# Division of the exponentials of two more batches moved to GpSimd, in a sliding-window attention with a GELU layer

## The chip, the cores and the metric

The kernel runs on one core of a Trainium2 chip. The metric is the device time of one execution in microseconds (us). Engines are called TensorE (PE; its weight loads PEld), VectorE (DVE), ScalarE (ACT), GpSimd (POOL) and SyncE (SP, which issues the DMAs).

## What is computed

```python
# q, k, v: [8, 8, 576, 64] (batch, head, position, feature); w_in [512, 2048], w_out [2048, 512], all float32
scores = scale * np.matmul(q, k.transpose(0, 1, 3, 2))
mask = (rel >= 0) & (rel < 128)                       # rel = query position - key position
scores = np.where(mask, scores + bias[None], -1e9)    # bias: -slope of the head * rel
attn = np.exp(scores - np.max(scores, axis=-1, keepdims=True))
attn = attn / (np.sum(attn, axis=-1, keepdims=True) + 1e-09)
x = np.matmul(attn, v)                                # to [4608, 512]: heads side by side
h = x @ w_in
out = 0.5 * h * (1.0 + erf(h / sqrt(2))) @ w_out      # float32
```

## The kernel before

**Numbers as halves.** Most products are made in float16 with three terms: each float32 operand is scaled by a power of two and split into a high half (the value rounded to float16) and a low half (the rest); high by high, low by high and high by low are added in PSUM. `low_part` (L334, one VectorE instruction at L335) makes a low half as source x scale - high.

**Attention, by units.** A unit is one batch and one pair of heads: 8 x 4 units. A unit's scores are 9 groups of 128 rows (two heads' or two blocks' queries, 64 each) by 192 keys. The steps of a unit of batch 1 or later: `scores` (L634, matmuls of 64 rows into PSUM), `biased` (L686: VectorE scales and adds the bias into `s`, float32 in SBUF; GpSimd fills masked stretches at L699), then for the groups 0 to 4 and 5 to 8 apart `softmax` (L776: maxima at L781, one exponential a group on ScalarE at L785 with its row sum, reciprocal of the sums at L788 and L789, then the division), `low_weights` (L799: the low halves and the transpose, a DMA from `e_main` to `et` at L809), at last `weigh` (L826: matmuls of `et` with the halves of v, L854) and `leave` (L862: two halves of x). `e_main` is one tile for all units, `s` and `et` are two each.

**The division has two forms**, chosen by a letter for each batch in `HALVES` (L36). Form "a" (L792): ScalarE copies each group with the scale 1/sum to the high half in `e_main`, and VectorE makes its low half from `s`, the scale and the high half, group by group (L808, recorded as L335). Form "w": GpSimd multiplies each group of `s` by 1/sum in place (L795); ScalarE casts all 5 or 4 groups at once to the high halves (L797); VectorE subtracts these from `s` in one instruction (L805). Batch 0 is done in float32 in another way and ignores its letter. Before, batches 1 and 2 have form "a" and batches 3 to 7 form "w".

**The layers.** Tiles of 512 tokens go through w_in (L904 in the first tiles; later in seven smaller products with precomputed sums, L1133), GELU on ScalarE, halves (GpSimd or ScalarE high, VectorE low) and w_out (L950, L947 in float32 for tile 0, L1283 for the last tiles). The precomputed sums are written to DRAM and loaded again. From batch 3's time on `qbuf`, `kbuf`, `vbuf` and `e_main` hold q, k, v and the exponentials, and at the end, when the attention is over, sums of weights.

**The order is written out.** Each piece of work is a generator, and each `next` of it (a step) issues its instructions. `ORDER` (L62) lists the steps of the whole kernel, 3570 of them, and the engines get their instructions in that order. The first digit is a stage, then come a letter and the unit or part: `0M30` is a step of `softmax` of batch 1, unit 3, groups 0 to 4, `0N30` one of its `low_weights`, `0Y3` its weighing; batch 2 has `02M30`, `02N30` and `02Y3`, batch b from 3 on the digit b - 1 (`4M30` for batch 5). `0z0` to `0z2` load q and k of batch 0, `0F` w_in, `0H3` is a part of the first layer's product, `0g3` its GELU. `PSUM_BANKS` and `ROOMS` say which PSUM bank and which output room each request gets, in the order of the requests. Engines wait for each other by semaphores, set from the tiles that each instruction reads and writes.

**Places.** Tiles in SBUF lie in the order in which they are first asked for, each rounded up to 32 bytes a partition. `one` (L287) is a tile of one element for a matmul that spreads a maximum over the partitions (L300). In the program of the kernel before `qbuf` begins at byte 6688 of each partition, `kbuf` at 15904, `vbuf` at 25632 and `e_main` at 35872.

Of the kernel before, what the change touches and what calls it, by code (L numbers as in the profile page):

```python
# [11 lines left out]
F32 = mybir.dt.float32  # L12
# [23 lines left out]
HALVES = "aaawwwww"  # L36
# [31 lines left out]
0n20 0j0 0n20 0n20 0t1 0e1 0x30 0t1 0n21 0t1 0n21 0a1 0p0 0w0 0e1 0e1 0t1 0e1 0t1 0e1 0z 0p0 0j1 0t2 0t2 0F 0p0 0p0
0n30 0z 0z 0v0 0p0 0W0 0e2 0e2 0F 0n30 0p0 0j1 0m31 0n21 0t2 0e2 0t2 0n21 0j1 0F 0n21 0t2 0F 0F 0e2 0v0 0W1 0L1 0v0
0v0 0i0 0a2 0m31 0v0 0e2 0v0 0n30 0n30 0n30 0n30 0x31 0a2 0i0 0l0 0l0 0L0 0i1 0w1 0l1 0l1 0w2 0H1 0x31 0H1 0t3 0t3  # L70
0x31 0x31 0n31 0H0 0n31 0H0 0i1 0l2 0a3 0H2 0n30 0n31 0n31 0t3 0n31 0n31 0l2 0a3 0j2 0p1 0a4 0a4 0j2 0e3 0e3 0e3 0t3
0t3 0H3 0H3 0p1 0e3 0e3 0H1 0p1 0p1 0w3 0H2 0j4 0a5 0j5 0W3 0j2 0p1 0d 0l3 0j4 0F 0p1 0W2 0L2 0lv 0lv 0lv 0H3 0i2 0a5
0p2 0f 0l3 0H2 0H0 0lv 0i2 0L3 0f 0j3 0H1 0p0 0g1 0p2 0H2 0g2 0p2 0p2 0H4 0j4 0H3 0p2 0j5 0p2 0j3 0H5 0H5 0H4 0p1 0j6
0a6 0a7 0j7 0H4 0H4 0p2 0i4 0i4 0H5 0H5 0g5 0H8 0H8 0H8 0H8 0g8 0j3 0H9 0H9 0H9 0H9 0g9 0j5 0i5 0i3 0H0 0g0 0v1 0a7
0a6 0p3 0i5 0H10 0A0 0i3 0A1 0J1 0H10 0J0 0H11 0j6 0H11 0H11 0p3 0v1 0H6 0H11 0g11 0H7 0v1 0j6 0H6 0p3 0p3 0H10 0H10
0p3 0p3 0i6 0p3 0v1 0v1 0v1 0u1 0cl 0H6 0cl 0j7 0f 0cl 0g3 0i6 0A2 0J2 0H7 0H7 0H7 0g7 0H12 0H12 0H13 0H13 0j7 0H12
0H12 0g4 0A1 0g12 0H13 0H13 0i7 0i7 0lq 0q1 0H15 0H15 0g10 0A0 0A2 0H6 0J0 0J0 0lq 0J1 0J1 0H14 0v1 01c 0H14 0H14 0H14
# [129 lines left out]
def attention_gelu_mlp(  # L207
# [10 lines left out]
    nc = tc.nc  # L218
# [68 lines left out]
    one = pool.tile([1, 1], F32, name="one")  # L287
# [1229 lines left out]
```

## Time and profile before

| what | us |
|---|---|
| median of 3 runs | 874.44 (871.98 to 876.07) |
| profiled execution, its time | 873.86 |
| profiled execution, its span (first to last instruction) | 872.1 |
| TensorE busy | 842.9 (97%) |
| VectorE busy | 706.8 (81%) |
| ScalarE busy | 612.0 (70%) |
| GpSimd busy | 342.9 (39%) |

The profile is one execution. Busy times are unions of the engine's instructions; matmuls overlap, so a busy TensorE is one that always has a matmul under way. The clock granted to TensorE is full (1.00) but for the last window, after the last matmuls. Batches 1 and 2 fill the stretch from about 100 to 250 us, the other batches that up to about 720 us; after that only the layers of the last tiles are left.

### The profile page before, as it was taken

The numbers are of one execution on the slowest core, as the hardware profiler recorded it, in microseconds if no ns is written. First come the engines' busy times: TensorE is split into PE (matmuls) and PEld (weight loads), VectorE is DVE, ScalarE is ACT, GpSimd is POOL, SyncE is SP. The second block draws the span as 40 slices with busy tenths as digits, with TensorE's granted clock in tenths as the row PEclk, the third lists the DMA queues.
The fourth block names the chain that finished last, engine by engine and source line by source line (L and its number), as shares of the span: only waits on it lengthen the run. The fifth ranks groups of instructions, "written<-read, shape, count | busy, mean of one in ns | idle before, by whom it ended". The sixth has DMA issues, their size and how long they took to land.

```text
span 872.1 us, 19752 instructions
## 1 busy us (share of the span) xinstructions
PE 842.9 (97%) x7876; PEld 549.3 (63%) x7876; DVE 706.8 (81%) x1275; ACT 612.0 (70%) x1234; POOL 342.9 (39%) x553
## 2 busy tenths in 40 slices
PE   7899999999999999999999998998999999999997
PEld 4644444544544455884578556864587467888886
DVE  5998999899889966889797988799778656784772
ACT  6978879888769967775677776764776547753671
POOL 5731000033024774479635965576435670000000
PEclk9999999999999999999999999999999999999999
DMA  9855666642563557555846396447752493412301
GB/s 306 286 161 201 230 188 116 152 161 57 102 144 98 137 133 207 194 128 150 188 143 187 104 212 177 127 86 188 187 188 56 110 200 152 188 50 85 110 1 50
DMA packets 180940, 129.47 MB, mean 148 GB/s; under 512 B 134384, under 2 KB 157040, under 8 KB 177136
## 3 DMA queue, kind: packets, MB, share of 16 engines
q1 hardware_dynamic: 180848, 128.21, 53.3%
q8 instruction: 62, 1.02, 0.5%
q14 instruction: 30, 0.25, 0.1%
HBM read 75.89 MB, written 17.83 MB: 107 GB/s over the span
## 4 chain that ended last, share of the span: by engine, by line
PE 55%; DVE 19%; DMA 10%; ACT 8%; issue 4%; POOL 3%; SPq 0%; DVEq 0%; ACTq 0%; POOLq 0%
PE u L1133 12%; PE v L1133 9%; PE h L904 9%; DMA et<-e_main 7%; PE o L950 6%; PE o L947 5%; PE u_out L1283 4%; DMA k<-kp 3%; DVE g L335 3%; PE sc L667 3%; DVE s L693 2%; DVE e_main L805 2%; DVE nmax L781 2%; PE av L854 1%; PE z_out L1283 1%
## 5 line engine op out<-in xcount | busy, mean ns | idle before, releaser
L950 PEld LDWEIGHTS <-g 128*128 128x128 f16 x1152 | 111.0, 98 | 131.2
L950 PE MATMUL o<-wo,g 128*128 128x512 f16 x864 | 192.2, 379 | 0.0
L785 ACT ACTIVATE s<-s,nmax 128x192 f32<-128x192 f32 x252 | 112.0, 446 | 46.8 <-DVE nmax L781 46.5
L904 PE MATMUL h<-x,wi 128*128 128x512 f16 x576 | 128.6, 379 | 1.9 <-DVE wi L335 1.6
L795 POOL TENSOR_SCALAR s<-s,z 128x192 f32<-128x192 f32 x180 | 100.9, 576 | 25.0 <-DVE z L789 11.5
L1133 PEld LDWEIGHTS <-t 128*128 128x128 f16 x1008 | 98.4, 98 | 11.8
L904 PEld LDWEIGHTS <-wi 128*128 128x128 f16 x576 | 54.8, 98 | 67.8 <-DVE wi L335 1.9
L1133 PEld LDWEIGHTS <-wi 128*128 128x128 f16 x864 | 83.9, 98 | 13.4 <-issue 1.3
L699 POOL MEMSET s<- 64x128 f32 (+1 forms) x112 | 19.3, 173 | 157.2 <-DVE s L693 143.6
L693 DVE SCALAR_TENSOR_TENSOR s<-sc,cs,bias_h 128x384 f32<-128x384 f32 x112 | 65.6, 606 | 2.0 <-PE sc L667 1.1
L950 PE MATMUL o<-wo_moved,g 128*128 128x512 f16 x288 | 66.0, 379 | 0.0
L781 DVE TENSOR_REDUCE nmax<-s 128x5 f32<-128x960 f32 (+1 forms) x56 | 58.4, 1047 | 3.4 <-POOL s L699 2.5
L1133 PE MATMUL u<-xs,t 128*128 128x256 f16 x504 | 59.9, 273 | 0.0
L947 PE MATMUL o<-zo,g 128*128 128x512 f32 x128 | 57.6, 599 | 0.0
L854 PE MATMUL av<-et,vbuf 128*64 128x128 f16 (+2 forms) x1392 | 43.7, 220 | 13.7 <-DMA et<-e_main 13.7
L805 DVE TENSOR_TENSOR e_main<-s,e_main 128x960 f16<-128x960 f32 (+1 forms) x40 | 46.5, 1168 | 11.4 <-ACT e_main L797 11.3
L667 PE MATMUL sc<-kbuf,qbuf 64*64 64x192 f16 (+3 forms) x1656 | 49.3, 251 | 6.3 <-DMA kbuf<-kp 4.6
L854 PEld LDWEIGHTS <-vbuf 128*64 128x64 f16 x1392 | 40.3, 111 | 23.4 <-issue 17.9
L1184 POOL TENSOR_SCALAR g<-rooms,sg 128x512 f16<-128x512 f32 x48 | 39.5, 830 | 24.7 <-ACT rooms L1178 21.5
L785 ACT ACTIVATION_READ_ACCUMULATOR s<-s,nmax 128x1 f32 x252 | 47.7, 189 | 0.0
L335 DVE SCALAR_TENSOR_TENSOR g<-rooms,sg,g 128x512 f16<-128x512 f32 x48 | 40.6, 864 | 8.0 <-POOL g L1184 7.9
L797 ACT CAST e_main<-s 128x960 f16<-128x960 f32 (+1 forms) x40 | 36.1, 907 | 14.5 <-POOL s L795 10.4
(256 smaller groups left out, 1698.6 us busy)
## 6 DMA issues: line engine op xcount, KB each, us to landing
t<-stored SPq DMA_DIRECT2D x21, 1024.0 KB, 5.2
v<-vp SPq DMA_DIRECT2D x32, 320.0 KB, 5.4
out<-ob SPq DMA_DIRECT2D x34, 256.0 KB, 2.8
raw<-w_in SPq DMA_DIRECT2D x8, 1024.0 KB, 10.7
raw<-w_out SPq DMA_DIRECT2D x8, 1024.0 KB, 6.1
q<-qp SPq DMA_DIRECT2D x7, 1152.0 KB, 5.8
k<-kp SPq DMA_DIRECT2D x7, 1152.0 KB, 7.1
stored<-sums SPq DMA_DIRECT2D x8, 512.0 KB, 2.7
```

Source lines behind the costliest of these rows:

```text
L335: return nc.vector.scalar_tensor_tensor(out=dst, in0=src, scalar=scale, in1=high, op0=ALU.mult, op1=ALU.subtract)
L667: done = nc.tensor.matmul(ps[bank][o, n, gap:W], a, m[:, gap:W], start=(i == 0 and (n == 0 or b > 0)), stop=(i == len(terms) - 1 and b > 0 ...
L693: yield nc.vector.scalar_tensor_tensor(out=s[:, bank[0] : bank[0] + k, :], in0=ps[bank][:, 0:k, 0:W], scalar=cs, in1=bias.broadcast_to([P, ...
L781: yield nc.vector.tensor_reduce(out=nmax[:, r], in_=s[:, r], axis=AX.X, op=ALU.max, negate=True)
L785: yield nc.scalar.activation(s[:, i, :], s[:, i, :], AF.Exp, bias=nmax[:, i : i + 1], accum_out=z[:, i : i + 1])
L795: yield nc.gpsimd.tensor_scalar(to, s[:, i], z[:, i : i + 1], 1.0, op0=ALU.mult, op1=ALU.mult)
L805: yield engine.tensor_tensor(out=e[:, r, 1, c], in0=st.s[:, r], in1=e[:, r, 0, c], op=ALU.subtract)
L854: done = nc.tensor.matmul(av[r, (js[0] - blocks[0]) * QB : (js[-1] + 1 - blocks[0]) * QB], v32s[b][:, hp, kb, r] if b < EXACT else vbuf[:, ...
L904: done = nc.tensor.matmul(ph, wi[n][:, a, cc, k * P : (k + 1) * P], x[:, cc, b, :], start=(i == 0), stop=(i == 3 * NCC - 1),)
L947: done = nc.tensor.matmul(o, g[:, r, c], zo[n][:, n % 2, k * DM : (k + 1) * DM], start=(fc == first), stop=(fc == last))
L950: done = nc.tensor.matmul(o, g[:, r, a, c], (wo if t else wo_first)[n][:, b, k, :], start=(fc == first and i == 0), stop=(fc == last and i ...
L1133: done = nc.tensor.matmul(ps[:, k * HT : (k + 1) * HT], w(a, i)[:, k * P : (k + 1) * P], m(b, i), start=first and n == 0, stop=True, skip_ ...
```

## The change

`HALVES` gives batches 1 and 2 the letter "w". Their nine scaled copies and nine scaled subtractions a unit become nine divisions on GpSimd, two casts and two subtractions. The instructions of all other work are the same. `ORDER` (now 3530 steps), `PSUM_BANKS` and `ROOMS` are replaced as a whole, from the first load on. The tile `one` and its memset are asked for behind `e_main`, so that `pww`, `sww`, `qbuf`, `kbuf`, `vbuf` and `e_main`, with the small tiles between them, lie 32 bytes lower; what comes behind keeps its place unless it is first asked for in another order.

```diff
-HALVES = "aaawwwww"
+HALVES = "awwwwwww"
...
 ORDER = """
-0z0 0z0 0z0 0b 0b 0b 0b 0s0 0z1 0z1 0m00 0s0 0x00 0z2 0z2 0F 0z1 0m00 0x00 0x00 0x00 0m00 0x00 0s0 0z2 0z2 0m01 0m01
...
-8r4 8r8 8r7 8I 8r8 8I 8I 8r8 8r8
...
+4M30 4N20 4Y1 4v 4M30 4M30 4d2 4M30 4M21 4M21 4M21 4Y0 4Y1 4M21 4v 4B3 4M31 4M30 4o2 4M30 4M30 4M30 4M30 4M30 4M30 4X0
...
 PSUM_BANKS = (
-    "0123456701234567015267340152671352713521321567340256402624013640176475126350674350435043504350450450"
...
+    "0123456701234567015672307416253205257453274502136721367231250124027164230045610745045704570457045704"
...
 ROOMS = (
-    "20201200120220110101012021012012001201201200210211210210211201012012021020120101201210202102"
+    "20120120102120220211201210212012020112122102102101212102121002021021021212012120121021210210"
 )
...
     nc.vector.memset(square, 0.0)
-    one = pool.tile([1, 1], F32, name="one")
-    nc.vector.memset(one, 1.0)
...
     e_main = pool.tile([P, NG, 2, 256], F16, name="e_main")
+    one = pool.tile([1, 1], F32, name="one")
+    nc.vector.memset(one, 1.0)
```

## Rows read from the trace of the kernel before

**Rows 1.** The page, its first part: busy us of each engine, share, instructions.
```profile
PE 842.9 (97%) x7876; PEld 549.3 (63%) x7876; DVE 706.8 (81%) x1275; ACT 612.0 (70%) x1234; POOL 342.9 (39%) x553
```

**Rows 2.** Stretches of the span: busy us of each engine, clock, DMA share, GB/s.
```profile
0.00:40.00 40.00, 31.39 (x369) 22.65 (x370) 31.14 (x75) 32.39 (x97) 24.96 (x53) 1.00 0.98 322
100.00:250.00 150.00, 146.74 (x1262) 72.84 (x1254) 139.06 (x316) 121.69 (x288) 20.19 (x49) 1.00 0.58 137
860.00:880.00 20.00, 7.10 (x66) 6.12 (x63) 3.04 (x5) 0.69 (x1) 0.00 (x0) 0.88 0.15 50
```

**Rows 3.** Groups of TensorE, 0 to 40 us (busy, mean ns, idle before).
```profile
L667 PE MATMUL sc<-kbuf,qbuf 64*64 64x192 f32 x144 | 10.6, 377 | 5.4 <-DMA kbuf<-kp 4.6 <-ACT s L733 0.8
L904 PE MATMUL h<-x,wi 128*128 128x512 f16 x7 | 2.2, 380 | 1.9 <-DVE wi L335 1.6 <-DVE x L335 0.3
```

**Rows 4.** Waits (us in total, times, longest), then L854's groups, 100-350 and 350-720 us.
```profile
PE av L854 <- DMA et<-e_main: 13.7, 10, 2.9
DVE e_main L805 <- ACT e_main L797: 11.3, 9, 3.0
ACT e_main L797 <- POOL s L795: 10.4, 8, 3.1
...
L854 PE MATMUL av<-et,vbuf 128*64 128x64 f16 (+2 forms) x624 | 18.6, 218 | 3.3 <-DMA et<-e_main 3.2
...
L854 PE MATMUL av<-et,vbuf 128*64 128x128 f16 (+2 forms) x726 | 23.6, 221 | 10.4 <-DMA et<-e_main 10.4
```

**Rows 5.** Timeline of TensorE around single waits: start us, length us, work [idle before, releaser].
```profile
164.47 1.58 PE L854 MATMUL av<-et,vbuf 128*64 128x256 f16 x54 [1.00 <-DMA et<-e_main]
...
228.49 2.06 PE L854 MATMUL av<-et,vbuf 128*64 128x128 f16 x66 [0.80 <-DMA et<-e_main]
...
249.11 1.54 PE L854 MATMUL av<-et,vbuf 128*64 128x128 f16 x42 [1.45 <-DMA et<-e_main]
...
533.08 1.59 PE L854 MATMUL av<-et,vbuf 128*64 128x128 f16 x60 [2.95 <-DMA et<-e_main]
```

**Rows 6.** Groups by shape over the whole span: busy us, mean ns, idle before.
```profile
L792 ACT ACTIVATE e_main<-s,z 128x192 f16<-128x192 f32 x72 | 27.6, 445 | 5.4 <-DVE z L789 2.4 <-DMA et<-e_main 1.6 <-DVE z L788 1.2
L335 DVE SCALAR_TENSOR_TENSOR e_main<-s,z,e_main 128x192 f16<-128x192 f32 x72 | 26.7, 414 | 4.6 <-ACT e_main L792 4.3
L797 ACT CAST e_main<-s 128x960 f16<-128x960 f32 x20 | 19.7, 987 | 4.0 <-POOL xr L1059 1.7 <-POOL s L795 1.4 <-DVE square L306 0.9
L797 ACT CAST e_main<-s 128x768 f16<-128x768 f32 x20 | 16.5, 827 | 10.4 <-POOL s L795 9.0 <-DMA et<-e_main 1.2
L805 DVE TENSOR_TENSOR e_main<-s,e_main 128x960 f16<-128x960 f32 x20 | 25.3, 1263 | 3.3 <-ACT e_main L797 3.2
L805 DVE TENSOR_TENSOR e_main<-s,e_main 128x768 f16<-128x768 f32 x20 | 21.5, 1074 | 8.1 <-ACT e_main L797 8.1
L795 POOL TENSOR_SCALAR s<-s,z 128x192 f32<-128x192 f32 x180 | 100.9, 576 | 25.0 <-DVE z L789 11.5 <-DVE z L788 7.7 <-ACT rooms L1174 2.3
```

**Rows 7.** Instructions of L795: shortest, median, longest in ns.
```profile
L795 POOL TENSOR_SCALAR s<-s,z x180: 418/427/2987, 270.3 to 710.3; 128x192 f32<-128x192 f32 x180
```

**Rows 8.** Timeline of GpSimd, then of VectorE beside its 4.11 us.
```profile
410.21 4.11 POOL L795 TENSOR_SCALAR s<-s,z 128x192 f32<-128x192 f32 x5 [0.16 <-DVE z L789]
...
500.44 2.16 POOL L795 TENSOR_SCALAR s<-s,z 128x192 f32<-128x192 f32 x2
...
409.96 0.71 DVE L335 SCALAR_TENSOR_TENSOR g<-m,sg,g 128x512 f16<-128x512 f32 x1
...
411.31 1.22 DVE L1040 TENSOR_TENSOR wsums<-wsums 128x1024 f16<-128x1024 f32 x1
```

**Rows 9.** Stretches from a unit's scores to its landing: batch 1 and batch 5, unit 3.
```profile
133.70:164.30 30.60, 29.76 (x216) 14.55 (x216) 28.19 (x94) 27.85 (x56) 0.29 (x2) 1.00 0.78 152
...
498.70:532.90 34.20, 30.74 (x312) 17.13 (x311) 30.34 (x62) 24.47 (x47) 25.48 (x33) 1.00 0.80 180
```

**Rows 10.** Instructions of L809: the transposes' time from issue to landing.
```profile
DMA to landing us min/median/max: 4.2/5.0/9.0
```

More of the change, by code (lines that the diff above doesn't have):

```diff
@@ L68 @@
[L68 to L77, printed above, removed]
@@ new lines @@
+01g13 03Q 01g13 01g8 01g8 02M11 03Q 02M01 02M11 02M11 01H9 01o3 01H14 01H14 02S2 02M01 03V 03V 02M11 01g15 01g15 01g9
+01g9 02N01 02N01 02S2 01g11 02S2 02N00 01o2 02N00 02B2 01g11 01g11 02M11 02M11 02B2 02B2 02B2 03V 03V 01g9 01g14 02B2
+02M11 02M11 03Q 02B2 02B2 02B2 02B2 02M11 03V 03V 01o1 01g14 02M20 02M11 02M11 01o1 01o1 02S3 02S3 03Q 03Q 03Q 03Q
+02M20 02S3 03V 03V 03V 02M20 02M20 02M20 02N11 02M20 01g15 02M21 03Q 01g14 02M10 02M10 03Q 03Q 03Q 02M20 02N10 02N10
+02N11 02B3 02B3 02B3 02B3 02M21 02M21 02M21 02M21 02M21 02M21 02M21 02M21 01o1 01k1 01o2 01o2 02M20 02M20 02M20 02B3
@@ new lines @@
+3M30 3X1 3v 4gs 3v 3M21 3M21 3M30 3M30 3M30 3M30 3M30 3X1 3M31 3X1 3M21 3N21 3M31 3X1 3Z0 3o2 3Z0 3o2 3o2 3o2 5gs 3N21
+3M31 3M31 3M31 3M31 3q 3q 3q 3M31 3M31 3M31 3X0 3X0 3M31 3M31 3q 3q 3q 3q 3Z0 3M30 3Z0 3N30 3q 3q 3q 3M31 3q 3q 3q 3q
+3q 3q 3o3 3Y2 3N30 3N31 3k2 3N31 5gs 3Z0 3k2 3Y2 3q 3q 3q 3q 3q 3X2 3Z0 3Z0 3Y3 3Y3 3X3 3o3 3X3 3X3 3X2 4T0 3X2 3X2
+3X3 3Z1 3Z1 4T1 3k3 3k3 4S0 4B0 4B0 4B0 4B0 4B0 4U 413 410 4a0 3Z1 3Z1 3Z1 3Z1 4a1 4B0 4B0 4M00 4M00 4M00 4M00 4M00
+412 3k0 4M00 3Z1 4B0 4B0 4M01 4M01 4M00 4M00 4M00 420 4a0 4a2 421 4a1 4M01 461 4M00 4U 4M01 4M01 4M01 4M01 4M01 460
@@ new lines @@
+5c2 5e1 5e1 531 5c1 5M00 5N00 572 5e0 5M01 5N01 5N01 5d2 552 5d2 542 5e0 5N00 523 5c1 5c1 5d2 5a1 5e2 5e0 5d1 5a3 5c0
+5c0 5V 5V 5V 5V 5c1 5a3 5a2 563 5c3 5a3 5a3 5c0 5d2 5a2 5e2 532 5c2 5c2 5c2 5S1 5B1 573 5B1 5B1 5B1 5B1 5B1 5B1 553
+5d3 5d3 5d3 5d3 5B1 543 5e3 5e2 5M10 533 5c3 5c3 5a2 L 5B1 5M11 L L L 5M10 5Y0 5M11 L L 5M10 5M10 5S2 5B2 5M10 5M10
+5B2 5B2 5B2 5M11 5M11 5B2 5B2 5B2 5B2 5B2 5o1 5X0 5o1 5e3 5c2 5S3 5M10 5M10 5c3 5M10 5M10 5M10 5M10 5M20 5M11 5M11
+5M11 5X0 5M20 5M20 5M20 5M11 5M11 5M11 5M11 5M20 5M20 5v 5v L 5v 5v 5v 5v 5M20 5o0 5M21 5M20 5M10 5v L L 5v 5M20 5M10
@@ new lines @@
+5N31 5X2 5X2 5Y3 5Y3 6T1 5X3 5X3 5k2 5X2 5X2 5X3 6S0 5X3 610 6a0 5Z0 6B0 6B0 6B0 6B0 613 6B0 6B0 6a3 6T0 6M00 6M00
+6M00 6M00 611 6M00 5Z1 5Z1 5Z1 621 7gs 5Z1 5Z1 6B0 6B0 6a1 6a1 5Z1 5Z1 612 6B0 6M00 6M01 620 6a0 6M00 623 6M00 660
+6M00 6U 6U 6T2 6c0 6M00 622 6M01 6M01 5k3 6M01 6M01 6a0 6a0 6M01 6M01 651 661 5k2 6c1 6M01 6a3 670 6d0 650 6M01 6M01
+6M00 6a1 6a1 671 6d0 6d0 6d1 6M00 6M00 6d0 6d1 640 6T3 630 6e0 6a1 6d1 6M00 6a0 6a2 631 6c0 6c0 641 6d0 6e0 6e0 662
+6a2 652 663 6M01 6M01 6N01 6c2 6c1 6c1 6c1 6c1 6c0 6c0 6a2 6a2 6a3 6c3 672 6d2 7gs 6a2 653 6d2 6d2 6d2 673 6d3 6N00
@@ L193 @@
+8E 8e3 8e3 8e3 8f3 8f3 8D 8G 8D 8f3 8D 8I 8f3 8B 8e3 8e3 8D 8r3 8r4 8I 8f2 8f2 8C 8r2 8F 8F 8F 8F 8r5 8f3 8G 8G 8I 8G
+8r2 8r6 8r6 8I 8r7 8r7 8r8 8r8 8r8 8r8
 """
 PSUM_BANKS = (
[L195 to L197 removed]
```

229 lines of the change are left out of this document (108 added, 121 removed).

## The prediction

> **What bounds the kernel now.** I read the busy time of each engine first [rows 1]. TensorE is busy 842.9 of 872.1 us. The change leaves every matmul as it is, so only the 29.2 us in which TensorE stands idle can be won, and the reader should find out where they lie before looking at anything else. The stretches of the span [rows 2] say: 8.61 us in the first 40 us, 3.26 us from 100 to 250 us, and in the last 20 us window TensorE works for 7.10 of some 12.1 us, so about 5.0 us are the tail of stores. The rest, about 12.3 us, lies between 250 and 720 us. Of the first 8.61 us, 4.6 are the first load and 1.9 the wait for the first halves of w_in [rows 3].
>
> The waits by what ended them [rows 4] name the rest: the weighing matmuls (L854) waited ten times, 13.7 us in all, for the DMA transpose of the exponentials (et<-e_main). 3.3 us of these lie between 100 and 350 us, where batches 1 and 2 (the second and third, counted from 0) are done, and 10.4 us after 350 us, in batches 4 to 7, whose instructions the change does not touch. Single waits are 1.00, 0.80 and 1.45 us in batches 1 and 2, and up to 2.95 us later [rows 5].
>
> So VectorE is not the bound, though it comes second: from 100 to 250 us it is busy 139.06 of 150 us, ScalarE 121.69, GpSimd only 20.19 [rows 2]. It matters through latency: a unit's last weighing needs scores, bias, maximum, exponentials, division, halves and transpose, and all of that has to end while TensorE does other work.
>
> **The change part by part.** Batches 1 and 2 have 8 units of 9 groups, 72 groups in all.
>
> What is removed: on ScalarE 72 copies with a scale, 27.6 us busy, and on VectorE 72 scaled subtractions, 26.7 us busy [rows 6]. What is added, by the same operations of batches 3 to 7: on ScalarE 8 casts of 960 and 8 of 768 elements, 8 x (0.987 + 0.827) = 14.5 us; on VectorE 8 subtractions of each size, 8 x (1.263 + 1.074) = 18.7 us [rows 6]; on GpSimd 72 divisions. So ScalarE is relieved of 13.1 us and VectorE of 8.0 us. Neither is at the end of the path: TensorE had 3.26 us of idle time in that stretch, and that is all this relief can bring there.
>
> GpSimd's divisions are 427 ns at the median, but up to 2987 ns [rows 7], and a mean of 560 (100.9 us for 180) [rows 6]. Five in a row beside VectorE's two-input operations at L335 and L1040 took 4.11 us, 0.82 each [rows 8]. The 72 divisions thus cost GpSimd between 30.7 us (72 x 0.427) and 59.2 us (72 x 0.822). It has about 130 us free there [rows 2], so its own time costs nothing; what counts is the chain. I take the mean, 0.56.
>
> The chain of one half of a unit, from the reciprocal to the transpose. Before: five copies, 27.6 / 72 = 0.38 each, the last subtraction behind them, 0.41: 2.3 us. After: five divisions, 5 x 0.56 = 2.8, one cast 0.99, one subtraction 1.26: 5.05 us. With four groups: 1.9 before, 2.24 + 0.83 + 1.07 = 4.1 after. A wide cast can't start before the last division, and a wide subtraction not before the cast ends; the narrow ones ran in step. So each half gets later by 2.2 to 2.8 us in this sum, by 1.6 us if GpSimd is undisturbed (5 x 0.427), and by nothing where the half lies ahead of need. Behind the waiting cast on ScalarE stand the exponentials of the next half and the activations of the first layer; behind the waiting subtraction on VectorE stand the next bias and low parts; TensorE's weighing and, through x, the next first-layer products wait for these. In the batches that already work in this way the casts waited 10.4 us for the divisions (8 times) and the subtractions 11.3 us for the casts (9 times) [rows 4].
>
> The order, the banks and the rooms are made anew for the whole kernel, not only for two batches. This decides more than the rest, since most of the idle time lies elsewhere. Every step of the order stands for a known piece of work. I gave each step the time of its instructions in the trace (the new steps: the rows above), and for each of the 28 units of batches 1 to 7 I summed TensorE's work and VectorE's work from the end of its scores to its first weighing. The stretches of the trace agree with the sums of the order before: for batch 1, unit 3, TensorE 29.76 (sum 29.8) and VectorE 28.19 (31.8) of 30.60 us; for batch 5, unit 3, 30.74 (30.7) and 30.34 (31.6) of 34.20 us [rows 9]. The margin is TensorE's work less VectorE's: where it is small, the weighing comes before its transpose.
>
> In the order before, 11 units have a margin under 6 us, and these waited 11.5 us in all, 1.05 each; the other 17 waited 2.1 us, 0.13 each (nearly all of it one transpose of batch 4 that took 9.0 us to land [rows 10]). In the new order the margin grows from -2.0 to 8.6 (batch 1, unit 3), 5.9 to 16.3 (batch 2, unit 1), 5.8 to 8.0 (batch 2, unit 3), -0.9 to 4.0 (batch 5, unit 3) and 3.8 to 13.4 (batch 7, unit 3). It shrinks from 8.6 to 1.5 (batch 4, unit 0), 7.0 to -2.6 (batch 6, unit 3) and 12.0 to 6.4 (batch 7, unit 1). Seven units stay under 6 us; the longer chain takes some 1.8 us more from those of batches 1 and 2 and puts two more under it. At 1.05 and 0.13 us each that is 7 x 1.05 + 21 x 0.13 = 10.1 us to 9 x 1.05 + 19 x 0.13 = 11.9 us of waiting in place of 13.7: between -3.6 and -1.8 us. I take -2.7.
>
> The start. Up to the first product with w_in VectorE has 34.6 us of work by the new order and 33.5 by the old one, TensorE 28.2 in both; the same loads keep the DMA engines at a share of 0.98 [rows 2]. Between 0 and +1.1 us; some of the later work takes its place, so I take 0. The end keeps its last products and stores: 0.
>
> The tile of ones. It takes one slot of 32 bytes a partition ahead of w_in's scales, qbuf, kbuf, vbuf and e_main. In the program before these four begin 32 bytes past a multiple of 256 (e_main at 35872); without the slot they begin on one (35840). Its own memset, one element, stays where it was among the first instructions of VectorE, give or take the memsets ahead of it: nothing. Whether the start of e_main matters to a transpose no row shows, since all 56 read the same tile. I bound it by the landings: 4.2 at the least, 5.0 at the median [rows 10]. [...] No row is nearer to one end than to the other; I take 0, as long as no row shows an effect, and keep -8 for the range.
>
> Sum: -2.7 us on the profiled execution, whose time is 873.86 us with a span of 872.1: 871.2 us. That execution lies 0.6 us under the median of the three runs (874.44), so the forecast for the median is 871.7 us.
>
> **The rivals.**
>
> First, the tables only move the waits (0.27): TensorE's work is the same, the new margins under 6 us give waits of the size of the old ones, and the time is 874.4, give or take 2 us. For it: batch 4, unit 0 and batch 6, unit 3 lose 7.1 and 9.6 us. Against it: five of the old waits gain more.
>
> Second, on the other side (0.18): GpSimd is held up by VectorE. The mechanism is that of the 4.11 us row: a division that meets a VectorE operation with two SBUF inputs takes 0.82 us, and VectorE is 93% busy from 100 to 250 us with such work. Two in a row have taken 2.16 us, 1.08 each [rows 8]. At that a half of five is later by 5 x (1.08 - 0.427) + 1.8 = 5.1 us. Units 1 and 2 of batch 1 and unit 3 of batch 2, weighed as soon as they landed in the order before, gain margins of 4.9, 3.9 and 2.2 us, so they are short by 0.2, 1.2 and 2.9 us, together 4.3. VectorE waits for GpSimd in turn, half a division (0.21 us) at each of five, 1.1 us on each of the three units: 3.2 more. With none of the 2.7 won that is 874.4 + 7.5 = 881.9 us. It decides from a mean division of about 0.8 us, where the half is later by 3.8 us. [...]
>
> Third, the start of e_main shortens the transposes (0.12): all land as the fastest do, 0.8 us sooner, and each of the ten waits gets shorter: 871.7 - 8 = 863.7 us at the most, 866 if half of it counts. Against it: the transposes that meet no wait gain nothing. [...]
>
> Fourth, the two units that lose margin stop TensorE for as much as they lose beyond the old wait, half of 7.1 + 9.6 (0.06): +8.4 - 2.7, about 880 us.
>
> **How the numbers follow.** My forecast, small shorter waits, has 0.37: 871.7, by itself 868 to 874. The rivals have 0.27 (872 to 876), 0.18 (876 to 884), 0.12 (863 to 868) and 0.06 (878 to 882). The range reaches to the alignment below and into the held-up GpSimd above: 864 to 880. A measurement of this kernel can tell about 0.5% from no change, 4.4 us: faster is under 870.1. Under it lie the third case and a good half of my own: 0.34. Above 878.8 lie most of the second and the fourth: 0.19. In between 0.47.
>
> **What would show it.** Right: L795 has 252 divisions, L792 none; VectorE loses some 8 us and ScalarE 13; the waits of L854 for et<-e_main sum to 10 to 12 us; TensorE's busy time stays within 1 us of 842.9. [...] Alignment: transposes that land in under 4.2 us at the least and well under 5.0 at the median. Moved waits: single waits of 3 us or more at batch 4, unit 0 or batch 6, unit 3. I would be wrong outright if TensorE's idle time in the first 40 us grew or shrank by more than 2 us, since I take it as unchanged, or if a wait other than the transposes' came up behind the casts.

## The result and the profile after

The kernel after takes 853.02 us (852.77 to 854.06), beside 874.0 us for the kernel before on the same chip: a ratio of 0.976, with a 95% interval of 0.974 to 0.979. The forecast was 871.7 with a range of 864 to 880. The time lies 11 us below the range.

The page of after, its first part, as in [rows 1] (lines of after stand two to four lower than those of before: L793 is the division, L795 the cast, L803 the subtraction, L807 the transpose, L852 the weighing):

```profile
PE 839.7 (99%) x7876; PEld 548.6 (64%) x7876; DVE 702.7 (82%) x1219; ACT 588.8 (69%) x1172; POOL 368.2 (43%) x625
```

Stretches of before that [rows 2] did not show (columns as there), then those of after:

```profile
350.00:720.00 370.00, 357.70 (x3719) 245.18 (x3717) 305.73 (x527) 248.88 (x524) 225.99 (x345) 1.00 0.60 155
```

```profile
0.00:40.00 40.00, 32.28 (x370) 22.64 (x371) 31.25 (x75) 32.05 (x97) 21.46 (x54) 1.00 0.98 320
100.00:250.00 150.00, 149.90 (x1278) 75.01 (x1278) 133.29 (x259) 108.98 (x233) 55.31 (x125) 1.00 0.48 131
250.00:350.00 100.00, 99.29 (x936) 51.94 (x934) 84.53 (x147) 77.86 (x149) 59.74 (x88) 1.00 0.56 153
350.00:700.00 350.00, 349.08 (x3614) 238.40 (x3613) 297.80 (x513) 238.63 (x517) 218.18 (x342) 1.00 0.57 157
```

TensorE's idle time was 29.2 us (872.1 less 842.9) and is 12.6 (852.3 less 839.7). It fell from 3.3 to 0.1 us in batches 1 and 2 (100 to 250 us), from 12.3 to 0.9 in the later batches (350 us to the end of attention), from 8.6 to 7.7 at the start and from 5.0 to 3.2 at the end, and it rose from 0.1 to 0.7 between 250 and 350 us. Its busy time fell by 3.2 us with the same 7876 matmuls; by the groups of both traces that lies in the scores (49.3 to 47.8) and the weighing (43.7 to 42.2). It does not go with the waits alone: e1 below loses most of them and is busy for 842.4 us, e2 for 840.3. 16.6 and 3.2 are the 19.8 us between the two spans.

Some of the 21 us go with the clock granted to TensorE. Of the eight executions of the kernel before that were timed beside e1 to e4, two had a mean granted clock of 1.00 and took 870.5 and 870.8 us, and four had 0.994 and took 873.7 to 876.2; those of after had 0.999 or 1.000. At 1.00 the two kernels thus lie 16 to 18 us apart.

Waits of after, as in [rows 4], and the instructions of the transposes (ns at the least, median, most of the issue on SP's queue; then the time from issue to landing, as in [rows 10]):

```profile
PE av L852 <- DMA et<-e_main: 0.4, 1, 0.4
ACT e_main L795 <- POOL s L793: 21.6, 16, 4.3
DVE e_main L803 <- ACT e_main L795: 21.4, 13, 5.9
```

```profile
L807 SPq DMA_TRANSPOSE et<-e_main x56: 1317/2428/5687, 119.7 to 700.2; - x56
DMA to landing us min/median/max: 3.6/4.2/8.1
```

The same line of before:

```profile
L809 SPq DMA_TRANSPOSE et<-e_main x56: 1541/3066/5885, 119.2 to 713.0; - x56
```

So ten waits of the weighing, 13.7 us, became one of 0.4. The casts and subtractions wait about twice as long as before (10.4 and 11.3 us), and yet the weighing hardly waits. At the median a transpose takes 0.64 us less to issue and lands 0.8 us sooner.

### The profile page after: what moved, and what is told of

It is laid out like the page before. It is cut to its first block, busy times and chain, and to the rows that moved or that the text cites. A ratio compares the mean times of both kernels' runs of the same rounds, so it can differ in the third digit from the quotient of the medians.

```text
span 852.3 us, 19731 instructions
## 1 busy us (share of the span) xinstructions
PE 839.7 (99%) x7876; PEld 548.6 (64%) x7876; DVE 702.7 (82%) x1219; ACT 588.8 (69%) x1172; POOL 368.2 (43%) x625
## 4 chain that ended last, share of the span: by engine, by line
PE 59%; DVE 3%; DMA 2%; issue 1%; ACT 1%; POOL 0%; ACTq 0%; DVEq 0%; POOLq 0%
PE o L948 22%; PE u L1131 14%; PE v L1131 10%; PE u_out L1281 4%; PE av L852 3%; PE sc L663 2%; DMA et<-e_main 2%; PE z_out L1281 1%; PE x_out L1281 1%; PE v_out L1281 1%; PE y_out L1281 1%; DVE g L331 1%; DVE e_main L803 0%; ACT e_main L795 0%; DVE s L689 0%
## 5 line engine op out<-in xcount | busy, mean ns | idle before, releaser
L793 POOL TENSOR_SCALAR s<-s,z 128x192 f32<-128x192 f32 x252 | 142.0, 579 | 62.8 <-DVE z L787 45.1
L1131 PEld LDWEIGHTS <-t 128*128 128x128 f16 x1008 | 98.2, 98 | 12.3 <-DMA t<-stored 0.3
L1131 PEld LDWEIGHTS <-wi 128*128 128x128 f16 x864 | 84.0, 98 | 13.1 <-issue 0.8
L803 DVE TENSOR_TENSOR e_main<-s,e_main 128x960 f16<-128x960 f32 (+1 forms) x56 | 61.6, 1106 | 21.8 <-ACT e_main L795 21.4
L795 ACT CAST e_main<-s 128x960 f16<-128x960 f32 (+1 forms) x56 | 50.5, 906 | 35.4 <-POOL s L793 21.6
L663 PE MATMUL sc<-kbuf,qbuf 64*64 64x192 f16 (+3 forms) x1656 | 47.8, 252 | 4.9 <-DMA kbuf<-kp 4.6
L331 DVE SCALAR_TENSOR_TENSOR g<-rooms,sg,g 128x512 f16<-128x512 f32 x48 | 42.8, 910 | 7.9 <-POOL g L1182 7.6
L1182 POOL TENSOR_SCALAR g<-rooms,sg 128x512 f16<-128x512 f32 x48 | 37.5, 789 | 26.6 <-ACT rooms L1176 17.9
L852 PEld LDWEIGHTS <-vbuf 128*64 128x64 f16 x1392 | 39.6, 111 | 7.8 <-issue 6.9
L852 PE MATMUL av<-et,vbuf 128*64 128x64 f16 (+2 forms) x1392 | 42.2, 220 | 0.5 <-DMA et<-e_main 0.4
## 6 DMA issues: line engine op xcount, KB each, us to landing
raw<-w_in SPq DMA_DIRECT2D x8, 1024.0 KB, 11.2
```

The costliest lines, as they stand in the source:

```text
L663: done = nc.tensor.matmul(ps[bank][o, n, gap:W], a, m[:, gap:W], start=(i == 0 and (n == 0 or b > 0)), stop=(i == len(terms) - 1 and b > 0 ...
L793: yield nc.gpsimd.tensor_scalar(to, s[:, i], z[:, i : i + 1], 1.0, op0=ALU.mult, op1=ALU.mult)
L803: yield engine.tensor_tensor(out=e[:, r, 1, c], in0=st.s[:, r], in1=e[:, r, 0, c], op=ALU.subtract)
L852: done = nc.tensor.matmul(av[r, (js[0] - blocks[0]) * QB : (js[-1] + 1 - blocks[0]) * QB], v32s[b][:, hp, kb, r] if b < EXACT else vbuf[:, ...
L1131: done = nc.tensor.matmul(ps[:, k * HT : (k + 1) * HT], w(a, i)[:, k * P : (k + 1) * P], m(b, i), start=first and n == 0, stop=True, skip_ ...
```

## Experiments

Three things change: the place of `e_main`, the tables, and the form of division in batches 1 and 2. The first theory was that the place, which the forecast had put at nothing, carries the gain; the rival, that the tables do. Six kernels, with before and after, make all eight combinations.

**e1: the place alone.** Before, with `one` behind `e_main`, so that `qbuf`, `kbuf`, `vbuf` and `e_main` begin on multiples of 256 bytes.

```diff
-    one = pool.tile([1, 1], F32, name="one")
-    nc.vector.memset(one, 1.0)
...
     e_main = pool.tile([P, NG, 2, 256], F16, name="e_main")
+    one = pool.tile([1, 1], F32, name="one")
+    nc.vector.memset(one, 1.0)
```

> The kernel before with the tile of ones alone moved behind e_main, so that qbuf, kbuf, vbuf and e_main begin on a multiple of 256 bytes; division, order, banks and rooms as before. Before takes 874.0 us, after 853.0. Theory of the place (transposes land 0.8 us sooner, and each of the ten weighing waits gets shorter by it): 864 to 868 us, transposes at a median of 4.2 us, waits of L854 for et at 6 to 9 us in place of 13.7. Theory of the tables (the order alone took the waits away): 872 to 876 us, waits unchanged. If the transposes' speed explains everything, 853 us.

Measured: 862.95 us, ratio 0.988 (0.984 to 0.991). Its transposes, and the wait of the weighing:

```profile
L809 SPq DMA_TRANSPOSE et<-e_main x56: 1396/2524/6407, 119.4 to 705.3; - x56
DMA to landing us min/median/max: 3.6/4.2/8.5
```

```profile
PE av L854 <- DMA et<-e_main: 2.9, 4, 1.1
```

32 bytes less in front of `e_main`, and the waits fall by 10.8 us, the time by 10.3 from the 873.2 of before, timed beside e1 to e4. That is more than the theory of the place expected (864 to 868 us, waits of 6 to 9).

**e2: all but the place.** After, with `one` where it was before.

```diff
+    one = pool.tile([1, 1], F32, name="one")
+    nc.vector.memset(one, 1.0)
...
     e_main = pool.tile([P, NG, 2, 256], F16, name="e_main")
-    one = pool.tile([1, 1], F32, name="one")
-    nc.vector.memset(one, 1.0)
```

> The kernel after with the tile of ones alone put back in its old place, so that the four tiles begin 32 bytes past a multiple of 256 again. Theory of the place: transposes back at 5.0 us, and as the slack before the weighings is 0.05 to 1.6 us for about ten units, some of them wait again: 855 to 860 us. Theory of the tables: 853 us, as after.

Measured: 860.76 us, ratio 0.985 (0.982 to 0.989). The first part of its page, its stretches and the wait of the weighing:

```profile
PE 840.3 (98%) x7876; PEld 549.1 (64%) x7876; DVE 704.4 (82%) x1219; ACT 589.8 (69%) x1172; POOL 368.1 (43%) x625
```

```profile
100.00:250.00 150.00, 146.73 (x1275) 73.34 (x1269) 132.11 (x255) 106.00 (x228) 52.31 (x122) 1.00 0.56 133
350.00:720.00 370.00, 366.79 (x3804) 252.35 (x3804) 312.01 (x534) 250.58 (x531) 220.67 (x345) 1.00 0.61 158
720.00:859.50 139.50, 136.34 (x1276) 121.96 (x1270) 89.92 (x136) 73.93 (x115) 0.00 (x0) 1.00 0.24 88
```

```profile
PE av L852 <- DMA et<-e_main: 5.1, 6, 2.4
```

Tables and form together give 12.4 us without the place. From 100 to 250 us TensorE works exactly as much as before (146.73 and 146.74 us); the gain is behind 350 us (366.79 and 357.70), in batches whose form is the same, and at the end (3.2 us of idle time in place of 5.0).

**e3: the tables alone, in the old form.** The steps of the new order that form a doesn't need are left empty.

```diff
-HALVES = "awwwwwww"
+HALVES = "aaawwwww"
...
             yield nc.scalar.copy(e[:, r, 0, c], s[:, r])
+        else:
+            yield None
...
-                yield low_part(e[:, i, 1, c], st.s[:, i], st.z[:, i : i + 1], e[:, i, 0, c])
+                low_part(e[:, i, 1, c], st.s[:, i], st.z[:, i : i + 1], e[:, i, 0, c])
+            yield None
```

(`one` stands in its old place.)

> New order, banks and rooms with the old division in batches 1 and 2 (copies by ScalarE in the divisions' places, narrow subtractions by VectorE in the wide one's) and the tile of ones in its old place. Theory of the tables: 856 to 862 us. Theory of the division (8 us less on VectorE and 13 us less on ScalarE made the room): 866 to 874 us, with VectorE busy again by some 8 us more and waits between 100 and 250 us.

Measured: 890.71 us, ratio 1.020 (1.015 to 1.024), far above both expectations. The wait of its scaled copies (L790), then stretches, then timelines of TensorE, VectorE and ScalarE:

```profile
ACT e_main L790 <- DMA et<-e_main: 26.8, 6, 9.3
```

```profile
120.00:140.00 20.00, 11.66 (x96) 5.60 (x96) 12.20 (x30) 9.21 (x35) 1.49 (x5) 0.74 0.58 119
350.00:720.00 370.00, 363.53 (x3755) 246.94 (x3755) 311.92 (x536) 252.29 (x527) 221.27 (x345) 1.00 0.61 160
```

```profile
134.18 1.17 PE L665 MATMUL sc<-kbuf,qbuf 64*64 64x192 f16 x23 [6.61 <-DVE stwo L299]
133.69 0.17 DVE L786 TENSOR_SCALAR z<-z 128x4 f32<-128x4 f32 x1 [7.46 <-ACT s L783]
131.30 1.15 ACT L790 ACTIVATE e_main<-s,z 128x192 f16<-128x192 f32 x3 [6.82 <-DMA et<-e_main]
```

The new order lets a unit's division begin while the transposes of the unit ahead still read `e_main`. GpSimd's division in place writes only `s` and may do so; a scaled copy writes `e_main` and holds ScalarE, 6.82 us here, with the exponentials behind it. VectorE then waits 7.46 us for these and TensorE 6.61. TensorE's clock, 1.00 from 120 to 140 us before, is granted at 0.74 in that stretch, and its busy time over the whole span is 849.0 us (842.9 before). Even so the later batches keep most of their gain (363.53 us of work from 350 to 720).

**e4: the form alone, with the old tables.** Five divisions' steps and four subtractions' are made to fit the old steps.

```diff
-HALVES = "aaawwwww"
+HALVES = "awwwwwww"
...
-            yield nc.gpsimd.tensor_scalar(to, s[:, i], z[:, i : i + 1], 1.0, op0=ALU.mult, op1=ALU.mult)
+            done = nc.gpsimd.tensor_scalar(to, s[:, i], z[:, i : i + 1], 1.0, op0=ALU.mult, op1=ALU.mult)
+            if st.b > 2 or i < r.stop - 1:
+                yield done
...
+            for _ in range(r.stop - r.start - 1 if st.b < 3 else 0):
+                yield None
```

> Old order, banks and rooms and the tile of ones in its old place; batches 1 and 2 alone divide on GpSimd, cast and subtract widely (the cast in the last copy's step, the subtraction in the last low half's). Theory of the division: 860 to 868 us. Theory of the tables: 874 to 880 us, since each half gets 1.6 to 2.8 us later in an order that was not made for it. GpSimd held up by VectorE: above 880 us, divisions of over 0.8 us on the mean.

Measured: 880.68 us, ratio 1.008 (1.005 to 1.011). Its casts (L799) and the stretch:

```profile
ACT e_main L799 <- POOL s L795: 32.7, 16, 4.6
```

```profile
100.00:250.00 150.00, 143.67 (x1186) 70.22 (x1179) 124.58 (x253) 105.21 (x226) 56.14 (x121) 0.99 0.51 129
```

In the old order the longer chain of a half is not free: TensorE loses 3.1 us against [rows 2] from 100 to 250 us, and the casts' wait for GpSimd grows from 10.4 to 32.7. Over the whole span of this execution it is idle for 1.4 us more than before and busy for 5.5 more (848.4), at a mean clock of 0.994; an execution of e4 at 1.00 took 878.6 us, so the loss is not the clock's alone.

**e5 and e6: the place added to e3 and to e4.** The edit is that of e1 on top.

```diff
     e_main = pool.tile([P, NG, 2, 256], F16, name="e_main")
+    one = pool.tile([1, 1], F32, name="one")
+    nc.vector.memset(one, 1.0)
```

> The new tables with the old form of division in batches 1 and 2, but e_main on a multiple of 256 bytes. If the place of e_main is worth the same wherever transposes end late (10 us on the kernel before, 8 us with the new tables and the new form, 8 us with the old tables and the new form), this kernel is 8 to 10 us faster than the same without the place (890.7): 881 to 883 us, with transposes landing at a median of 4.2 us. If most of the excess of the new tables with the old form is ScalarE's wait for the transposes of e_main (26.8 us there), the place takes a larger part of it: 875 us or less.

> Old order, banks and rooms, batches 1 and 2 divided on GpSimd, and the tile of ones behind e_main. The new division alone took 880.7 us, 7.5 more than before. If the place gives its gain to any order: 870 to 873 us. If it gives more where more waits: down to 866 us; if the division's waits hide it: 878 us or more.

Measured: e5 878.98 us, ratio 1.006 (1.004 to 1.008); e6 872.70, ratio 1.000 (0.998 to 1.002). With them the eight times are, in us:

| tables | form in batches 1, 2 | e_main 32 bytes past | e_main on a multiple | difference |
|---|---|---|---|---|
| old | a | 873.2 (before) | 862.95 (e1) | -10.3 |
| old | w | 880.68 (e4) | 872.70 (e6) | -8.0 |
| new | a | 890.71 (e3) | 878.98 (e5) | -11.7 |
| new | w | 860.76 (e2) | 853.02 (after) | -7.7 |

(The kernel before, timed beside each run, moved between 872.4 and 875.0. With each run taken against the one beside it the four differences are -10.3, -7.8, -12.9 and -8.5.) The place gives 8 to 13 us wherever it is added; in e5 it gave 11.7, between the two expectations. Tables alone lose 17.5 us, the form alone loses 7.5, and both together win 12.4: neither can be priced without the other.

**e7 and e8: which tile's place.** In e7 only `e_main` begins 32 bytes past a multiple of 256, in e8 only `e_main` begins on one.

```diff
     e_main = pool.tile([P, NG, 2, 256], F16, name="e_main")
-    one = pool.tile([1, 1], F32, name="one")
-    nc.vector.memset(one, 1.0)
```

In e7 `one` then stands right ahead of `e_main`; in e8 both stand behind `square`, `e_main` first.

> The kernel after with the tile of ones between vbuf and e_main: qbuf, kbuf and vbuf begin on a multiple of 256 bytes, e_main 32 bytes past one. If the source of the transposes is what counts: 860 to 862 us, as with the tile in its old place (860.8), transposes at 5.0 us. If the other three count (matmul operands, loads): 853 us, as after.

> The kernel after with e_main alone on a multiple of 256 bytes (placed ahead of the others) and qbuf, kbuf and vbuf 32 bytes past one. If the source of the transposes is what counts: 852 to 854 us, transposes at 4.2 us. If the other three count: 860 to 862 us.

Measured: e7 858.86 us, ratio 0.984 (0.981 to 0.987); e8 853.74, ratio 0.978 (0.976 to 0.981). The transposes of e7, then of e8:

```profile
L807 SPq DMA_TRANSPOSE et<-e_main x56: 1317/3006/5842, 121.0 to 707.6; - x56
```

```profile
L807 SPq DMA_TRANSPOSE et<-e_main x56: 1318/2436/6144, 119.7 to 699.6; - x56
```

What counts is the place of `e_main`, the source of the transposes; that of `qbuf`, `kbuf` and `vbuf` brings at most 2 us (e7 lies 1.9 us under e2, e8 0.7 above after).

**e9, e10 and e11: which boundary, and the destination.** After, with `e_main` 128 bytes (e9) or 64 bytes (e10) past a multiple of 256; in e11 both `et` tiles begin on multiples of 256 too (in after they begin 32 and 64 bytes past one).

```diff
+    pad = pool.tile([P, 32], F32, name="pad")
+    nc.gpsimd.memset(pad[0:1, 0:1], 0.0)
     e_main = pool.tile([P, NG, 2, 256], F16, name="e_main")
```

```diff
     e_main = pool.tile([P, NG, 2, 256], F16, name="e_main")
+    for k in range(2):
+        first = pool.tile([P, NG * 2, P], F32, tag=f"et{k}", name=f"first{k}", bufs=1)
+        nc.gpsimd.memset(first[0:1, 0, 0:1], 0.0)
```

(e10 has 16 in place of 32.)

> The kernel after with 128 bytes more ahead of e_main, so that it begins 128 bytes past a multiple of 256. By a rule of 256-byte boundaries the transposes stay slow: 5.0 us and about 861 us. By a rule of 64 or 128 bytes they stay fast: 4.2 us and about 853 us.

> The kernel after with e_main moved to 64 bytes past a multiple of 256. If only a start on a multiple of 256 bytes is good, it takes 859 to 861 us, as with 32 and 128 bytes, and the transposes take 3.0 us each at the median from issue to end and land after 5.0. If a start on a multiple of 64 bytes were enough, it would take 853 us with transposes of 2.4 us.

> The kernel after with the tiles that the transposes write (et of both parities) put right behind e_main on multiples of 256 bytes as well; in the kernel after they begin 32 and 64 bytes past one. If the start of the destination counts as that of the source does, the transposes land well under 4.2 us at the median and the time falls by the 1 to 2 us of waits that are left, to 851 to 852 us. If only the source counts, they land after 3.6 at the least and 4.2 at the median as before, and the time is that of the kernel after, 853 us.

Measured: e9 859.56 us (ratio 0.984, 0.982 to 0.987), e10 860.79 (0.985, 0.983 to 0.987), e11 854.21 (0.977, 0.975 to 0.980). The transposes of e9, of e10 and of e11, with the landings of the first two:

```profile
L809 SPq DMA_TRANSPOSE et<-e_main x56: 1317/3049/5442, 120.9 to 705.9; - x56
DMA to landing us min/median/max: 4.2/5.0/7.5
```

```profile
L809 SPq DMA_TRANSPOSE et<-e_main x56: 1317/3014/6726, 119.5 to 708.2; - x56
DMA to landing us min/median/max: 4.2/5.0/10.3
```

```profile
L810 SPq DMA_TRANSPOSE et<-e_main x56: 1330/2367/5986, 119.7 to 700.7; - x56
```

32, 64 and 128 bytes past are equally bad (medians of 3.01, 3.01 and 3.05 us in e7, e10 and e9, and kernels of 858.9 to 860.8 us), a multiple of 256 is good (2.43 us and 853.0 in after), and the destination brings nothing that can be measured (2.37 us and 854.21 in e11). Why the price is the same at all three places, and why it is gone at a multiple of 256, no run shows.

One caution: the first transposes of e7 and e9 are issued at 121.0 and 120.9 us, 1.2 to 1.3 later than in after, as in e2; those of e10 are not. In the profiled executions of e2, e7 and e9 the clock granted from 0 to 40 us is 0.96, in those of after and e10 1.00, so in these three traces a part of the difference is the start.

**e12: the chain of a half made longer.** After, with a second multiplication by a tile of ones behind each division of batches 1 and 2.

```diff
-            yield nc.gpsimd.tensor_scalar(to, s[:, i], z[:, i : i + 1], 1.0, op0=ALU.mult, op1=ALU.mult)
+            done = nc.gpsimd.tensor_scalar(to, s[:, i], z[:, i : i + 1], 1.0, op0=ALU.mult, op1=ALU.mult)
+            if 1 <= st.b <= 2:
+                done = nc.gpsimd.tensor_scalar(to, s[:, i], ones_p, 1.0, op0=ALU.mult, op1=ALU.mult)
+            yield done
```

> The kernel after, but in batches 1 and 2 each division on GpSimd is followed by a second multiplication of the same group in place, by a tile of ones: 72 more instructions on GpSimd, 30 us at the 0.42 us of the shortest divisions, and each half of five groups later by 2.1 us or more (2.9 at the mean of 0.58). This prices the chain of a half, and with it the case that GpSimd is held up. By the prediction's own account of that case, three units are short of margin by what the chain gets longer beyond 4.9, 3.9 and 2.2 us, here by about 5.7 (2.8 and 2.9), so 0.8, 1.8 and 3.5 us, and VectorE waits for GpSimd besides: 6 us or more, 859 us or above. If the new tables leave the units of batches 1 and 2 room for a chain of this length, the time is within 2 us of the kernel after (853 to 855). If they leave none, since units are weighed as soon as their transposes land, all eight units lose 2.1 to 2.9 us each: 17 us or more, 870 us or above.

Measured: 882.71 us, ratio 1.012 (1.011 to 1.014), 29.7 us above after. The group of the added operations, stretches, and two waits of TensorE:

```profile
L797 POOL TENSOR_SCALAR s<-s,ones_p 128x192 f32<-128x192 f32 x72 | 37.0, 514 | 6.7
```

```profile
100.00:250.00 150.00, 134.56 (x1118) 66.03 (x1117) 118.32 (x231) 92.96 (x205) 79.59 (x174) 0.99 0.41 110
250.00:350.00 100.00, 92.11 (x783) 45.88 (x781) 81.34 (x138) 73.58 (x147) 57.51 (x95) 0.95 0.48 122
350.00:728.00 378.00, 377.88 (x3927) 255.77 (x3926) 318.04 (x549) 259.63 (x546) 233.89 (x360) 1.00 0.58 162
```

```profile
175.34 1.58 PE L857 MATMUL av<-et,vbuf 128*64 128x256 f16 x54 [2.21 <-DMA et<-e_main]
270.94 2.77 PE L857 MATMUL av<-et,vbuf 128*64 128x128 f16 x42 [7.15 <-DMA et<-e_main]
```

37.0 us on GpSimd, which in after is busy 55.31 of the 150 us, leave TensorE idle for 23.3 us from 100 to 350 us in place of 0.8, and hardly at all behind that (0.1 us up to 728). 11.2 of the 23.3 are three waits of the weighing, the rest many small waits of other products. Its clock is 0.95 from 250 to 350 us, the stretch of the 7.15 us wait, and its busy time is 846.1 us in place of 839.7. The last of the three expectations came true, and by more: in the new order the chains of batches 1 and 2 have no room for this much more.

**e13 and e14: six table loads put back.** The traces with the new order show something that the text of the change doesn't: ScalarE loads an activation table (GELU's or the exponential's) whenever the function changes, and the new tables change it less often. Before, ScalarE goes from one of the two functions to the other 33 times, after 27 times; with a first load that is the 34 and 28 loads of the two traces. Before, three of its groups (form, count, busy us, mean ns):

```profile
L785 ACT ACT_TABLE_LOAD x16 | 20.5, 1283 | 3.4 <-DVE nmax L781 3.1
L1178 ACT ACT_TABLE_LOAD x8 | 10.3, 1283 | 0.1
L921 ACT ACT_TABLE_LOAD x7 | 9.0, 1283 | 3.4 <-issue 3.3
```

The same of after:

```profile
L783 ACT ACT_TABLE_LOAD x13 | 16.7, 1283 | 0.2
L1176 ACT ACT_TABLE_LOAD x6 | 7.7, 1283 | 0.1
L919 ACT ACT_TABLE_LOAD x6 | 7.7, 1283 | 4.1 <-issue 4.0
```

Six loads fewer, 7.7 us. Both runs put six back into after, by a GELU of one column ahead of the exponentials of three units: e13 in units weighed under 1 us after their transposes land, e14 in units weighed over 20 us after.

```diff
+            if (st.b, st.hp, part) in ((4, 3, 1), (5, 3, 1), (6, 3, 1)):
+                nc.scalar.activation(idle, idle, AF.Gelu, scale=1.0)
             for i in range(r.start, r.stop):
```

(e14 has (3, 0, 1), (5, 0, 1), (7, 0, 1).)

> The kernel after with one GELU of a single column put ahead of the exponentials of groups 5 to 8 of unit 3 in batches 4, 5 and 6; each brings a load of the GELU table and a load of the exponentials' table, 2 x 1.28 = 2.6 us on ScalarE, six loads in all as in the kernel before. In the trace of after these three units are weighed 0.96, 0.82 and 0.77 us after their last transpose lands. If the chain of a unit takes the whole delay, each costs 2.6 less its spare, 1.6 to 1.8 us, 5 us in all: 858 us. If the later groups' exponentials had room, or VectorE ends the chain anyway, 853 to 854 us. If the delay also reaches the units behind, 861 us or more.

> The same six loads in unit 0 of batches 3, 5 and 7, groups 5 to 8; these units are weighed 24, over 20 and 29 us after their last transpose lands. If a load costs only where its unit's chain is tight, 853 to 854 us. If it delays ScalarE's later work for the tight units as well, since ScalarE takes its instructions in order, up to 5 us more: 858 us.

Measured: e13 862.33 us, ratio 0.986 (0.982 to 0.990); e14 860.48, ratio 0.984 (0.980 to 0.987): 9.3 and 7.5 us above after (8.3 and 6.5 with each taken against the kernel before timed beside it). The longest waits of TensorE that are new or longer, in e13 and then in e14 (the last two of e14 were 0.7 and 0.4 us in after):

```profile
PE av L856 <- DMA et<-e_main: 5.9, 3, 3.3
```

```profile
PE u L1135 <- ACT rooms L1176: 3.1, 3, 1.3
PE o L952 <- ACT g L923: 1.7, 1, 1.7
PE av L856 <- DMA et<-e_main: 1.2, 1, 1.2
```

In the tight units the delay ends at their weighing, 5.9 us where 5 were expected; TensorE's busy time is 3.1 us longer besides (842.8), with a clock of 0.99 from 350 to 700 us, and with that the time reaches the third expectation. In the loose ones the time is above the 858 us expected, and the delay ends at other work that stands behind it on ScalarE: sums and GELUs for the layers. A load put in costs 1.1 to 1.6 us of the kernel, about as much as it lasts, and the spare of its own unit does not save it. So six loads can cost 6.5 to 9.3 us in this order. That the six that went away cost the order before as much is not shown: they lie elsewhere, and the new order was made as a whole. How much of the 12.4 us is theirs and how much is the order's besides stays open.

## Why the prediction was wrong, step by step

**What bounds the kernel** held: TensorE's waits for the transposes were the thing to win, and they went. That only idle time could be won did not hold in full: 3.2 of the 19.8 us are busy time.

**The tile of ones** was the first failure. "I take 0, as long as no row shows an effect": the effect is 8 to 13 us. The row that bounded it gave the size for one transpose (the median falls by 0.8 us, from 5.0 to 4.2; the shortest falls too, from 4.2 to 3.6), and the third rival described it, with a chance of 0.12. The -8 kept for the range, ten waits times 0.8 us, was no upper bound: e1 took 10.8 us from the ten waits. (Half of the 8 us is 867.7 us, not the 866 written there.) The issue itself is shorter by 0.54 us (3066 to 2524 ns), and in the trace of before 12 of the 28 units' last transposes start within 0.1 us of the end of the issue ahead of them, so they start sooner as well as landing sooner. From before to e1 the time from a unit's last score to its last landing falls by 1.14 us in the mean of the 28 units.

**The order** was the second: -2.7 us was forecast for tables and form, -12.4 measured (e2). The step that failed is the one from margins to waits: 7 to 9 units under 6 us at 1.05 us each and the others at 0.13, so 10.1 to 11.9 us of waiting, and all else unchanged. In e2, with transposes as slow as before, the weighing waits for 5.1 us. Of the 12.6 us between the spans of before and e2 (872.1 and 859.5), these waits are 8.6, TensorE's busy time 2.6, and the end, which was taken as 0, 1.8; other waits take 0.4 back.

The margins did not tell which units wait. Four of e2's six waits:

```profile
165.12 1.58 PE L852 MATMUL av<-et,vbuf 128*64 128x256 f16 x54 [0.81 <-DMA et<-e_main]
230.89 2.06 PE L852 MATMUL av<-et,vbuf 128*64 128x128 f16 x66 [0.48 <-DMA et<-e_main]
528.10 1.59 PE L852 MATMUL av<-et,vbuf 128*64 128x128 f16 x60 [2.38 <-DMA et<-e_main]
618.49 1.54 PE L852 MATMUL av<-et,vbuf 128*64 128x128 f16 x42 [0.84 <-DMA et<-e_main]
```

They stand before batch 1, unit 3 and batch 2, unit 1, whose margins were forecast at 8.6 and 16.3 us, and before batch 5, unit 3 (4.0) and batch 6, unit 3 (-2.6). Batch 4, unit 0, with 1.5, did not wait. Some of the margins were off themselves. After, from the end of the scores to the landing, for batch 2, unit 1, batch 5, unit 3 and batch 6, unit 3:

```profile
178.20:226.40 48.20, 48.20 (x324) 22.58 (x324) 44.34 (x84) 32.26 (x84) 22.83 (x49) 1.00 0.38 99
493.40:520.40 27.00, 27.00 (x268) 15.00 (x270) 23.51 (x51) 20.25 (x36) 15.36 (x27) 1.00 0.98 213
570.90:610.50 39.60, 39.60 (x266) 19.35 (x267) 33.89 (x74) 27.08 (x56) 26.92 (x43) 1.00 0.76 190
```

TensorE's work less VectorE's is 3.9, 3.5 and 5.7 us, where 16.3, 4.0 and -2.6 were forecast. (The sums go by steps in their order, the rows by time.) The second agrees, the others do not.

What in the new order took the waits away stays open. One part can be the table loads. The sums by step took each step's instructions as given. "The instructions of all other work are the same" is true of the program's text, not of the chip's: six table loads went away, which belong to no step. Their rows stood in the profile of before, 34 loads of 1283 ns, and the changes between GELU and exponentials in the new order could have been counted from it. e13 and e14 price six at 6.5 to 9.3 us, in other places.

**The chain of a half** was allowed up to 1.8 us of waiting; in the old order the new form costs 7.5 us (e4). How long a single half's chain got no run here measures alone. By its own rows, the prediction's 1.6 us for an undisturbed GpSimd is 2.1 with five groups (5 x 0.427, 0.99 and 1.26 less 2.3). That "by nothing where the half lies ahead of need" would cover most halves was wrong for the new order: e12 makes GpSimd's work for each group of batches 1 and 2 longer by 0.514 us and costs 29.7 us.

**Relief of the engines.** VectorE fell by 4.1 us (8.0 forecast), ScalarE by 23.2 (13.1 forecast; 7.7 of the rest are the loads), GpSimd rose by 25.3, under the 30.7 of the forecast's lower end, since its other work got shorter by some 16 us.

**The rivals.** That the tables only move the waits is refuted by e2. GpSimd held up by VectorE did not come; the division's mean over the span is what it was in [rows 6] (576 ns there; the prediction's 560 is the busy time over the count), and from 100 to 250 us, where a mean of about 0.8 us was to decide, the 72 divisions take 35.1 us, 0.49 each:

```profile
L793 POOL TENSOR_SCALAR s<-s,z 128x192 f32<-128x192 f32 x252 | 142.0, 579 | 62.8 <-DVE z L787 45.1 <-DVE z L786 7.0 <-ACT s L783 6.5
```

But its price was no exaggeration: e12 brings GpSimd's work for a group to 1.09 us (0.576 and 0.514), and costs four times the 7.5 us that the rival counted. That batch 4, unit 0 and batch 6, unit 3 would stop TensorE for some 8 us is refuted: the one wait left is batch 4, unit 0, 0.4 us, and e2 has 0.84 at batch 6, unit 3.

**What to look for.** Two of the signs named were seen: 252 divisions at L793, and landings under 4.2 at the least and well under 5.0 at the median, which was the sign for the place. TensorE's busy time left its band of 1 us (by -3.2), and the waits of the weighing came to 0.4 us where 10 to 12 were forecast. The idle time of the first 40 us kept within the 2 us named (8.6 to 7.7).

Little is left: outside the first load (4.6 us), the rest of the start (3.1) and the end (3.2) TensorE is idle for 1.7 us of 852.3. No experiment points to a version that would beat after by what can be measured.

## What to carry to other kernels

Look at where the source of a DMA transpose begins: 32 bytes of a tile of one element cost this kernel 8 to 13 us, and a row that can't show an effect is no reason to put it at nothing when the bound is larger than the rest of the sum. When an order is written out anew, count what the order itself creates, table loads among it, and don't price an order and the form it was made for one by one. In a kernel whose TensorE is busy for 99% of the span, more work on an engine that is idle nearly two thirds of a stretch can still cost most of its length (37.0 us on GpSimd cost 29.7).

## What the runs showed of the hardware

The DMA transpose of this kernel takes 2.4 to 2.5 us to issue and 4.1 to 4.3 to land, as medians of the traces, when its source begins on a multiple of 256 bytes, and 3.0 to 3.1 and 4.9 to 5.1 when it begins 32, 64 or 128 bytes past one; where the destination begins makes no difference that can be measured in the kernel's time (854.2 us in e11, 853.0 in after). A table load on ScalarE lasts 1.283 us each time, one comes with each change between GELU and the exponential (33 and 27 changes, 34 and 28 loads with the first), and TensorE's waits that follow from it can lie in work that has nothing to do with the unit it stands in (in e14 3.1 us in three waits of L1135, one of the layers' products).
